# Two waits for GpSimd copies and thirteen matrix steps issued as 64-row pairs, in a sliding-window attention and gMLP kernel

## The chip, the cores and the metric

One core of one Trainium2 chip runs the whole program. The metric is device time in microseconds of an execution; a profiled execution gives a trace beside it. TensorE is called PE, VectorE DVE, ScalarE ACT, GpSimd POOL and SyncE SP, as in the profile.

## The reference

For each of 8 batch elements, q, k and v have 8 heads of 576 positions by 64. Attention is causal with a window of 64; its output, heads side by side, goes through a gMLP block with a spatial gate.

```python
scores = scale * np.matmul(q, k.transpose(0, 1, 3, 2))
mask = (rel >= 0) & (rel < window)                  # rel = query position - key position, window = 64
attn = softmax of the masked scores                 # along the keys
x = heads side by side of np.matmul(attn, v)        # (8, 576, 512)
h = np.maximum(x @ w_in, 0.0)                       # (8, 576, 1024)
u, v = h[..., :512], h[..., 512:]
v_n = (v - mu) / np.sqrt(var + 1e-06)               # layer norm of each row
v_s = np.einsum('ts,bsd->btd', w_spatial, v_n) + b_spatial[None, :, None]
return (u * v_s) @ w_out
```

## The kernel before

The kernel plans 1096 steps and issues them in the order of a list written out by hand, `ORDER` (L18 to L148). An entry such as `G1_3:PE:1` names a step, the engine that issues it and the buffers or PSUM banks that it takes. Steps of one engine run in the order of the list; semaphores from the tile framework order them across engines, by data and by the reuse of buffers and of the eight PSUM banks (128 rows by 512 float32 each).

For batch element b the steps are these, with g for the half of the heads and u for a pair of heads within it:

- `ldq`, `ldk`, `ldv` (DMA issues on SP) bring q, k and v; `cq`, `ck` (POOL, some on DVE or ACT) cast q and k to float16; `tq`, `tk` (DVE, L436) transpose them.
- `cv{b}_{lo}` casts two of the four 128-row chunks of v into the tile hv (L467). `sl` and `su` copy its lower and upper 64 rows into hs, v shifted by 64 rows (L474, L481). On POOL the helper `cp` (L298) issues one instruction of 512 elements a chunk (L308), so cv2_2 and su3_2 are two instructions each.
- `S` computes scores in products over 32 rows of the array (L512), `S{b}_r` those of the last 64 queries (L583); `E` exponentiates them on ACT (L521, L593), `M` masks them on DVE (L524, L597), `Z` sums them over the keys by products with a matrix of ones that write 64 output rows each (L537, L606), `N` and `n` form 1/sum on ACT as exp(-ln) (L563, L565), `P` multiplies with v in products of 64 output rows (L548, L619), and `X` multiplies by 1/sum on DVE (L556, L627) and writes x.
- `V` is x times the right half of w_in, `Vr` its ReLU on ACT (L677), `Vb` and `Va` its layer-norm statistics on DVE (L679, L681); `L1`, `L2` on ACT make 1/sqrt(var + eps), and five steps `A{b}_{j}` apply the layer norm on DVE (L736), in the order A1_4, A1_2, A1_3, A1_1, A1_0 and A2_1, A2_2, A2_0, A2_3, A2_4. `U` and `Ur` are the left half of w_in and its ReLU (ACT, L765), `G` the spatial product, `Ge` the gate on DVE (L796), `O` the product with w_out, `Oe` its eviction on ACT (L654), `st` the store.

V, U and O of an index below 4 are four products of 128 rows, 128 output rows and 512 columns, accumulated in one bank; G is five of them (the last has 65 rows: 64 of v and one for the bias). All of these go through one helper, `mm` (L312), and stand in the profile at L318. The remainder of 64 positions has steps of its own: `V{b}_4` (L710, L713) writes 64 output rows of V for one batch element and, in the other 64 rows of the same bank, the output product of the batch element before; `U{b}_4` is at L757 and `G{b}_4` at L788.

`mm` can issue a product in two ways; the list of before uses only the second:

```python
        if e == "PE2":
            for h in (0, 1):
                nc.tensor.matmul(o[64 * h:64 * h + 64, :], w[:, 64 * h:64 * h + 64], x, start=start, stop=stop)
        else:
            nc.tensor.matmul(o, w, x, start=start, stop=stop)
```

A second table, `HOLD` (L159), names steps whose first instruction waits, beside its own inputs, for the end of another step (L860). Before, it has one entry: sl6_0 on POOL waits for the mask M5_00 on DVE.

Of the kernel before, what the change touches and what calls it, by code (L numbers as in the profile page):

```python
# [55 lines left out]
A1_3:DVE:5 A1_1:DVE:6 A1_0:DVE:7 S2_1:PE:7:3:4:6 U1_2:PE:2 G1_2:PE:5 tk3_1:DVE:0 M2_01:DVE  # L56
M2_00:DVE E2_110:ACT:1 Oe0_3:ACT E2_100:ACT:3 E2_101:ACT E2_111:ACT M2_11:DVE st0_4:DQ ldq3_0:DQ:7
G1_1:PE:1 ldq3_1:DQ:1 S2_r:PE:4:0:7:3 Ur1_2:ACT:0 ldq4_0:DQ:2 ldk3_0:DQ:0 E2_r0:ACT:0 G1_4:PE:6
Z2_00:PE:2 E2_r1:ACT Z2_01:PE:4 E2_r2:ACT Ge1_1:DVE:5 M2_10:DVE G1_3:PE:1 G1_0:PE:0 Ge1_4:DVE:6
cv2_0:POOL:0 cv2_2:POOL sl2_0:POOL:0 su2_2:DVE sl2_2:DVE su2_0:POOL cq3_1:POOL:1 cq4_0:POOL:2  # L60
ck3_0:POOL:3 E2_r3:ACT N2_00:ACT:4 M2_r:DVE N2_01:ACT:2 n2_01:ACT s42:ACT n2_00:ACT Ge1_3:DVE:7
Ge1_0:DVE:8 cq3_0:POOL:0 st0_0:DQ Ge1_2:DVE:9 Z2_r:PE:7 Z2_10:PE:3 N2_r:ACT:5 n2_r:ACT P2_10:PE:6
P2_00:PE:2 P2_r:PE:4 P2_01:PE:1 X2_r:DVE:0 N2_10:ACT:0 n2_10:ACT Z2_11:PE:7 N2_11:ACT:3 P2_11:PE:0
n2_11:ACT O1_2:PE:5 V2_4:PE:3 Vr2_4:ACT:3 Oe1_4:ACT:0 X2_00:DVE:0 X2_01:DVE X2_10:DVE:1 X2_11:DVE
O1_3:PE:4 Oe1_2:ACT:0 Oe1_3:ACT tq3_1:DVE:1 tk3_0:DVE:2 V2_3:PE:2 V2_2:PE:7 Vr2_3:ACT:0
tq3_0:DVE:3 S3_1:PE:1:6:0:3 Vr2_2:ACT:2 E3_110:ACT:3 E3_111:ACT V2_0:PE:5 Vr2_0:ACT:6 V2_1:PE:4
E3_100:ACT:0 Vr2_1:ACT:4 S3_0:PE:2:7:0:3 Vb2_3:DVE:3 Va2_3:DVE Vb2_2:DVE:2 M3_11:DVE Vb2_0:DVE:1
# [5 lines left out]
Ur2_3:ACT:1 su3_0:POOL cv3_2:POOL su3_2:POOL E3_r0:ACT:1 E3_r1:ACT E3_r2:ACT Z3_10:PE:5 Z3_11:PE:6
Z3_00:PE:2 Oe1_1:ACT N3_10:ACT:1 ldv4_1:DQ sl3_2:POOL cq4_1:POOL:3 ldv4_4:DQ:1 ldk4_1:DQ:4
A2_3:DVE:3 A2_4:DVE ldv4_2:DQ:0 st1_0:DQ ldq5_0:DQ:6 U2_0:PE:0 Ur2_0:ACT:2 ldv4_3:DQ st1_4:DQ
ldk5_0:DQ:1 E3_r3:ACT N3_11:ACT:5 n3_11:ACT N3_00:ACT:4 cv4_0:ACT:0 G2_3:PE:4 G2_1:PE:3 n3_00:ACT
n3_10:ACT M3_01:DVE tq4_0:DVE:4 tk4_0:DVE:5 G2_2:PE:7 G2_0:PE:5 Ge2_3:DVE:0 M3_r:DVE Ge2_1:DVE:1
Z3_r:PE:0 P3_10:PE:1 Z3_01:PE:6 P3_00:PE:4 P3_11:PE:2 N3_r:ACT:2 Ge2_2:DVE:2 P3_01:PE:3 P3_r:PE:7
# [127 lines left out]
def kernel(  # L206
# [643 lines left out]
    for s, eng, banks in CHOOSE(plan):  # L850
# [42 lines left out]
```

## Time and profile before

| what | value |
|---|---|
| median of 3 runs | 197.49 us (197.48 to 197.74) |
| profiled execution, its own time | 196.44 us |
| span of its trace, first to last instruction | 194.7 us |
| granted TensorE clock, mean | 1.00 |
| instructions | 7039 |
| HBM read and written | 32.79 MB, 9.44 MB |

The profiled execution took 1.74 us more than its span. A row of a timeline has the start and the length in us, the engine, the line, what is written and read, the shapes, how many instructions were merged, and in brackets idle time before them with what ended it. A product's shape `128*64 128x512` has 128 rows of the array, 64 output rows and 512 columns; LDWEIGHTS (PEld) loads its weights. Matmul ends in the trace are modelled, so the prediction goes by their starts. A row of a chain has start, length, engine, tile and line.

### The profile page before, as it was taken

What the parts mean: (1) busy time and instruction counts of PE and PEld (TensorE: products, weight loads), DVE (VectorE), ACT (ScalarE), POOL (GpSimd) and SP (SyncE); (2) the same over time, 40 slices, a digit from 0 to 9 for tenths busy, and PEclk for the clock granted to TensorE, in tenths of its full rate; (3) what the DMA queues carried; (4) which work ended last, traced back from release to release, by engine and by line L of the source; (5) the groups of instructions that cost most, each with busy time, mean ns of one, the idle gap of its engine ahead of it and who ended that gap; (6) DMA issues with size and microseconds to landing.
All of it is one profiled execution on the core that took longest, in us unless ns stands there. A gap on an engine that the chain in (4) does not pass through costs nothing.

```text
span 194.7 us, 7039 instructions
## 1 busy us (share of the span) xinstructions
PE 184.9 (95%) x2955; PEld 99.2 (51%) x2955; DVE 167.1 (86%) x315; ACT 152.8 (78%) x326; POOL 94.0 (48%) x161
## 2 busy tenths in 40 slices
PE   7598999999999999999999999999999999999992
PEld 5475356464545454464446445654556454544450
DVE  5999899999999999999999989999986876448530
ACT  2079689898978899999999789987998977704642
POOL 4085856677669956549946890497400000000000
PEclk9999999999999999999999999999999999999999
DMA  6999999999999988999799958079205000007245
GB/s 202 362 202 374 392 395 210 310 411 261 202 347 305 297 253 221 363 357 353 167 251 303 284 167 251 20 174 288 82 26 198 3 0 3 2 0 238 112 175 205
DMA packets 49570, 42.68 MB, mean 219 GB/s; under 512 B 38593, under 2 KB 38849, under 8 KB 49538
## 3 DMA queue, kind: packets, MB, share of 16 engines
q1 hardware_dynamic: 49314, 41.90, 71.1%
q8 instruction: 23, 0.38, 0.9%
q10 hardware_dynamic: 224, 0.33, 0.5%
q14 instruction: 9, 0.07, 0.1%
HBM read 32.79 MB, written 9.44 MB: 217 GB/s over the span
## 4 chain that ended last, share of the span: by engine, by line
PE 57%; DVE 27%; SPq 7%; DMA 4%; issue 2%; POOL 1%; ACT 1%
PE bank L318 42%; DVE st L679 4%; DMA nq<-in_q_dram 4%; DVE vn L736 4%; DVE qT L436 4%; DVE kT L436 3%; SPq L452 3%; PE bank L512 3%; DVE e L524 3%; DVE x L556 3%; PE bank L548 2%; PE bank L710 2%; PE bank L537 2%; PE bank L788 2%; DVE g L796 2%
## 5 line engine op out<-in xcount | busy, mean ns | idle before, releaser
L521 ACT ACTIVATE e<-bank 128x512 f16<-128x512 f32 x64 | 34.7, 600 | 9.7 <-PE bank L512 8.8
L318 PE MATMUL bank<-wspT,vn 128*128 128x512 f16 (+1 forms) x160 | 38.6, 380 | 0.0
L796 DVE TENSOR_TENSOR g<-bank,ru 128x512 f16<-128x512 f32 (+1 forms) x40 | 24.4, 624 | 12.1 <-PE bank L318 8.8
L318 PE MATMUL bank<-x,win 128*128 128x512 f16 x128 | 31.5, 380 | 0.0
L318 PE MATMUL bank<-wout,g 128*128 128x512 f16 x128 | 31.3, 380 | 0.0
L318 PE MATMUL bank<-win,x 128*128 128x512 f16 x128 | 30.8, 379 | 0.0
L677 ACT ACTIVATE vs<-bank 128x512 f16<-128x512 f32 (+1 forms) x40 | 23.2, 604 | 9.0 <-PE bank L318 6.5
L308 POOL CAST hq<-nq 128x384 f16<-128x384 f32 x39 | 23.1, 630 | 13.6 <-DMA nq<-in_q_dram 11.3
L654 ACT COPY ob<-bank 128x512 f32<-128x512 f32 (+1 forms) x39 | 22.8, 596 | 8.1 <-PE bank L318 7.8
L679 DVE BATCH_NORM_STATS2 st<-vs 128x6 f32<-128x512 f16 (+1 forms) x40 | 25.7, 667 | 1.2 <-ACT vs L677 1.1
L308 POOL COPY hs<-hv 64x512 f16<-64x512 f16 x36 | 24.4, 702 | 4.3 <-ACT hv L300 2.1
L308 POOL CAST hv<-nv 128x512 f16<-128x512 f32 x26 | 17.3, 681 | 16.5 <-DMA nv<-in_v_dram 9.5
L765 ACT ACTIVATE ru<-bank 128x512 f32<-128x512 f32 (+1 forms) x40 | 21.4, 567 | 3.7 <-PE bank L757 2.0
L318 PEld LDWEIGHTS <-vn 128*128 128x128 f16 (+1 forms) x160 | 15.0, 97 | 18.2 <-DVE vn L736 0.5
L524 DVE TENSOR_TENSOR e<-e,mask 128x1024 f16<-128x1024 f16 x32 | 23.9, 763 | 0.3 <-ACT e L521 0.2
L556 DVE TENSOR_TENSOR x<-bank,lz 128x512 f16<-128x512 f32 x32 | 20.3, 676 | 2.6 <-ACT lz L565 2.0
L436 DVE STREAM_TRANSPOSE kT<-hk 128x576 f32<-128x576 f32 x16 | 19.8, 1239 | 0.4 <-POOL hk L308 0.4
L436 DVE STREAM_TRANSPOSE qT<-hq 128x576 f32<-128x576 f32 x16 | 19.8, 1239 | 0.4 <-POOL hq L308 0.2
L565 ACT ACTIVATE lz<-lz 128x512 f32<-128x512 f32 x32 | 19.9, 642 | 0.3
L308 POOL CAST hk<-nk 128x384 f16<-128x384 f32 x33 | 17.0, 551 | 4.7 <-DMA nk<-in_k_dram 4.4
L318 PEld LDWEIGHTS <-x 128*128 128x128 f16 x128 | 11.9, 98 | 14.3 <-DVE x L556 0.5
L563 ACT ACTIVATE lz<-bank 128x512 f32<-128x512 f32 x32 | 18.3, 607 | 0.7 <-PE bank L537 0.4
(87 smaller groups left out, 272.7 us busy)
## 6 DMA issues: line engine op xcount, KB each, us to landing
nq<-in_q_dram SPq DMA_DIRECT2D x16, 576.0 KB, 6.9
nk<-in_k_dram SPq DMA_DIRECT2D x16, 576.0 KB, 7.2
nv<-in_v_dram SPq DMA_DIRECT2D x32, 256.0 KB, 6.5
out_dram<-ob SPq DMA_DIRECT2D x14, 512.0 KB, 4.0
wi<-in_moe_w_in_dram SPq DMA_DIRECT2D x4, 512.0 KB, 7.6
ws<-in_moe_w_spatial_dram SPq DMA_DIRECT2D x2, 576.0 KB, 9.3
nv<-in_v_dram SPq DMA_DIRECT2D x8, 128.0 KB, 6.2
wo<-in_moe_w_out_dram SPq DMA_DIRECT2D x2, 512.0 KB, 6.6
```

The source lines that it names most:

```text
L308: nc.gpsimd.tensor_copy(o[:, lo:lo + step], i[:, lo:lo + step])
L318: nc.tensor.matmul(o, w, x, start=start, stop=stop)
L436: d = add(f"t{name}{b}_{g}", ("DVE", 1.09), key, lambda e: nc.vector.transpose(qt.t[:, :].rearrange("p (i j) -> p j i", j=18), h.t[:, :].b ...
L521: ex.append(add(f"E{b}_{g}{u}{w}", ("ACT", 0.475), key, lambda e, u=u, w=w: nc.scalar.activation(e2[u].t[:, w, :], sc[2 * u + w].t[:, :], ...
L524: mins.append(add(f"M{b}_{g}{u}", ("DVE", 0.602), key, lambda e, u=u: nc.vector.tensor_tensor(e2[u].t[:, :, :], e2[u].t[:, :, :], mask[:, ...
L556: lambda e, u=u, ob=ob, lz=lz: nc.vector.tensor_tensor(x.t[:, u, :], ob.t[:, :], lz.t[:, :], ALU.mult),
L565: c = add(f"n{tag}", ("ACT", 0.09 + 0.00083 * n), key, lambda e: nc.scalar.activation(lz.t[:, 0:n], lz.t[:, 0:n], AF.Exp, bias=0.0, scale= ...
L654: lambda e: (nc.vector.tensor_copy if last else nc.scalar.copy)(view(), m.t[rows, 0:n]),
L677: rl = add(f"Vr{b}_{j}", ("ACT", 0.476), key, lambda e: nc.scalar.activation(vs.t[0:jn, :], m.t[0:jn, :], AF.Relu), deps=[pv], acq=[vs], u ...
L679: s1 = add(f"Vb{b}_{j}", ("DVE", 0.595), key + 0.02, lambda e: nc.vector.bn_stats(st6.t[0:jn, 0:6], vs.t[0:jn, :]), deps=[rl], acq=[st6], ...
L765: lambda e, m=m, ru=ru, n=n: nc.scalar.activation(ru.t[:, 0:n], m.t[:, 0:n], AF.Relu), deps=[pu], acq=[ru], uses=[m])))
L796: lambda e, m=m, g=g, ru=ru, n=n: nc.vector.tensor_tensor(g.t[:, 0:n], m.t[:, 0:n], ru.t[:, 0:n], ALU.mult),
```

## The change

Two entries join `HOLD`: cv2_2, the cast of the second half of v of batch element 2, waits for A1_0, the last of the five layer-norm applications of batch element 1; and su3_2, the copy of the upper rows of that half for batch element 3, waits for A2_4, the last of batch element 2's. Both run on POOL and wait for DVE.

Thirteen steps change their engine word from PE to PE2, so that `mm` issues each product as two of 64 output rows, with 64 columns of the weights each and the same moving operand: four G steps (five pairs each) and nine V, U and O steps (four pairs each), 56 pairs for 56 products. TensorE issues 56 more products and 56 more weight loads. All thirteen stand next to steps Z, P or V{b}_4, which write 64 output rows, or next to others of the thirteen.

In the list the entries su3_2, sl3_2 and cq4_1 now stand behind A2_3 and A2_4, since the table needs the step that is waited for to be issued first. No engine's own order of steps differs. The cut diff, line breaks of the list left as they fall:

```diff
-Z2_00:PE:2 E2_r1:ACT Z2_01:PE:4 E2_r2:ACT Ge1_1:DVE:5 M2_10:DVE G1_3:PE:1 G1_0:PE:0 Ge1_4:DVE:6
+Z2_00:PE:2 E2_r1:ACT Z2_01:PE:4 E2_r2:ACT Ge1_1:DVE:5 M2_10:DVE G1_3:PE2:1 G1_0:PE2:0 Ge1_4:DVE:6
...
-n2_11:ACT O1_2:PE:5 V2_4:PE:3 Vr2_4:ACT:3 Oe1_4:ACT:0 X2_00:DVE:0 X2_01:DVE X2_10:DVE:1 X2_11:DVE
+n2_11:ACT O1_2:PE2:5 V2_4:PE:3 Vr2_4:ACT:3 Oe1_4:ACT:0 X2_00:DVE:0 X2_01:DVE X2_10:DVE:1 X2_11:DVE
...
-V3_3:PE:1 cv4_2:POOL ck5_0:POOL:2 tk5_0:DVE:2 Vb3_0:DVE:2 U3_2:PE:3 U3_1:PE:4 S4_r:PE:6:5:7:0
+V3_3:PE2:1 cv4_2:POOL ck5_0:POOL:2 tk5_0:DVE:2 Vb3_0:DVE:2 U3_2:PE2:3 U3_1:PE2:4 S4_r:PE:6:5:7:0
...
-cv6_0:POOL:0 sl5_0:POOL:1 U4_0:PE:4 V4_3:PE:7 Vr4_3:ACT:4 U4_1:PE:0 Vb4_3:DVE:2 U4_2:PE:2
-E5_r3:ACT M5_r:DVE G3_1:PE:6 Va4_3:DVE Ge3_1:DVE:9 Z5_10:PE:3 Z5_01:PE:5 Ur4_1:ACT:4 L14:ACT:0
+cv6_0:POOL:0 sl5_0:POOL:1 U4_0:PE2:4 V4_3:PE2:7 Vr4_3:ACT:4 U4_1:PE2:0 Vb4_3:DVE:2 U4_2:PE2:2
+E5_r3:ACT M5_r:DVE G3_1:PE2:6 Va4_3:DVE Ge3_1:DVE:9 Z5_10:PE:3 Z5_01:PE:5 Ur4_1:ACT:4 L14:ACT:0
...
-V6_3:PE:3 E7_111:ACT S7_r:PE:5:2:7:0 V6_1:PE:4 E7_r0:ACT:1 E7_r1:ACT Vr6_3:ACT:6 Vr6_2:ACT:0
-G5_0:PE:6 st4_0:DQ st4_1:DQ E7_r2:ACT Vr6_1:ACT:2 E7_r3:ACT sl7_2:DVE M7_11:DVE Z7_00:PE:5
+V6_3:PE:3 E7_111:ACT S7_r:PE:5:2:7:0 V6_1:PE2:4 E7_r0:ACT:1 E7_r1:ACT Vr6_3:ACT:6 Vr6_2:ACT:0
+G5_0:PE2:6 st4_0:DQ st4_1:DQ E7_r2:ACT Vr6_1:ACT:2 E7_r3:ACT sl7_2:DVE M7_11:DVE Z7_00:PE:5
...
-HOLD = {"sl6_0": "M5_00"}
+HOLD = {"sl6_0": "M5_00", "cv2_2": "A1_0", "su3_2": "A2_4"}
```

More of the change, by code (lines that the diff above doesn't have):

```diff
@@ L72 @@
 A2_0:DVE:2 Ur2_2:ACT:3 Ur2_1:ACT:5 U2_3:PE:2 O1_0:PE:6 O1_1:PE:7 S3_r:PE:0:4:3:1 Oe1_0:ACT:1
[L73 to L78, printed above, removed]
+Ur2_3:ACT:1 su3_0:POOL cv3_2:POOL E3_r0:ACT:1 E3_r1:ACT E3_r2:ACT Z3_10:PE:5 Z3_11:PE:6 Z3_00:PE:2
+Oe1_1:ACT N3_10:ACT:1 ldv4_1:DQ ldv4_4:DQ:1 ldk4_1:DQ:4 A2_3:DVE:3 A2_4:DVE su3_2:POOL sl3_2:POOL
+cq4_1:POOL:3 ldv4_2:DQ:0 st1_0:DQ ldq5_0:DQ:6 U2_0:PE:0 Ur2_0:ACT:2 ldv4_3:DQ st1_4:DQ ldk5_0:DQ:1
+E3_r3:ACT N3_11:ACT:5 n3_11:ACT N3_00:ACT:4 cv4_0:ACT:0 G2_3:PE:4 G2_1:PE:3 n3_00:ACT n3_10:ACT
+M3_01:DVE tq4_0:DVE:4 tk4_0:DVE:5 G2_2:PE:7 G2_0:PE:5 Ge2_3:DVE:0 M3_r:DVE Ge2_1:DVE:1 Z3_r:PE:0
+P3_10:PE:1 Z3_01:PE:6 P3_00:PE:4 P3_11:PE:2 N3_r:ACT:2 Ge2_2:DVE:2 P3_01:PE:3 P3_r:PE:7
 Ge2_0:DVE:3 N3_01:ACT:0 n3_01:ACT ck4_1:ACT:0 X3_10:DVE:2 X3_00:DVE:3 n3_r:ACT S4_0:PE:0:5:1:6
```

## The prediction

> **What bounds the kernel now.** I read the page first, then the chain that ended last, then what TensorE (PE) waits for, then single engines' timelines where PE waits.
>
> ```profile
> PE 184.9 (95%) x2955; PEld 99.2 (51%) x2955; DVE 167.1 (86%) x315; ACT 152.8 (78%) x326; POOL 94.0 (48%) x161
> PE   7598999999999999999999999999999999999992
> DVE  5999899999999999999999989999986876448530
> ```
>
> PE is busy in nearly every slice, VectorE (DVE) almost as much until three quarters of the span. The question is where one holds the other. The chain, thinned to the places that the change touches:
>
> ```profile
> 52.72 2.85 DVE vn L736 x5
> ...
> 56.73 1.71 DVE e L524 x3
> ...
> 61.38 0.65 DVE er L597
> ...
> 64.67 1.87 DVE x L556 x3
> ...
> 75.64 3.48 DVE vn L736 x5
> ...
> 84.60 0.61 DVE x L556
> ```
>
> Up to 85 us the chain runs through DVE, and both groups of five layer-norm applications (A1 and A2, L736) lie on it. From 85.25 us it runs on PE to the last evictions. Within the stretch of 48 to 85 us PE's timeline has two waits for DVE that a bracket names, this one at the softmax sums of batch element 2's remainder and one at S4_0 (85.25, below):
>
> ```profile
> 62.06 0.30 PE L606 MATMUL bank<-er,ones 128*64 128x128 f16 x4 [0.32 <-DVE er L597]
> ```
>
> So a microsecond taken from DVE before 85 us reaches the end if PE gets its inputs earlier. After 85 us only what shortens PE counts, as long as the other engines keep up.
>
> **The change part by part.**
>
> *Two holds.* What is an application worth beside GpSimd (POOL) and without it? Stretches of A1, A2 and A3 (columns: length, then PE, PEld, DVE, ACT and POOL busy):
>
> ```profile
> 52.50:55.56 3.06, 3.06 (x75) 1.45 (x73) 3.06 (x7) 2.47 (x6) 3.00 (x6) 1.00 1.02 301
> 75.50:79.12 3.62, 3.62 (x51) 1.62 (x50) 3.62 (x7) 3.62 (x10) 3.56 (x7) 1.00 0.80 226
> 98.05:99.76 1.71, 1.71 (x9) 0.78 (x8) 1.70 (x6) 1.71 (x5) 0.00 (x0) 1.00 1.31 244
> ```
>
> With POOL idle (A3) five take 1.7 us; with POOL busy throughout (A1, A2) they take about 3.0 and 3.55. The holds keep POOL out of four of A1's five (the cast before cv2_2 still meets the first) and all of A2: DVE saves about 3.06 - 1.70 - 0.1 = 1.25 us at A1 and 3.6 - 1.7 = 1.9 us at A2. POOL's order, and where the held copies go:
>
> ```profile
> 52.29 1.84 POOL L308 CAST hv<-nv 128x512 f16<-128x512 f32 x3 [0.71 <-DMA nv<-in_v_dram]
> 54.09 1.95 POOL L308 COPY hs<-hv 64x512 f16<-64x512 f16 x3
> 57.92 4.46 POOL L308 CAST hq<-nq 128x384 f16<-128x384 f32 x6 [1.88 <-DVE e L524]
> ...
> 75.16 2.85 POOL L308 COPY hs<-hv 64x512 f16<-64x512 f16 x4
> 77.97 2.12 POOL L308 CAST hq<-nq 128x384 f16<-128x384 f32 x3
> 82.19 1.09 POOL L308 COPY hs<-hv 64x512 f16<-64x512 f16 x1 [2.12 <-ACT hv L300]
> ```
>
> Behind cv2_2 on POOL stand sl2_0, su2_0 and the q cast of 57.92. From cv2_2's first cast (52.9) to 56.04 is 3.2 us; released at about 54.3 they end at about 57.5, inside the 1.88 us gap, so the q cast keeps its time. Behind su3_2 stand sl3_2 and one q cast, which end at 80.09; 1.8 us later they end near 81.9, still before the copy of 82.19, which waits for ScalarE (ACT). PE reads these v tiles only behind the sums that wait for M2_r (61.38 above) and, for su3_2, behind the G2 products (below, 83.1). The next load into the buffer that cv2_2 frees, ldv5_0, stands two batch elements later. The displaced copies are hidden on POOL.
>
> They are not hidden from DVE. In 54.3 to 57.5 DVE now runs a transpose, then the masks M2 (L524), which had POOL idle before:
>
> ```profile
> 56.58 1.86 DVE L524 TENSOR_TENSOR e<-e,mask 128x1024 f16<-128x1024 f16 x3
> ...
> 74.54 1.09 DVE L524 TENSOR_TENSOR e<-e,mask 128x1024 f16<-128x1024 f16 x1
> ```
>
> Alone a mask takes 0.6 us of DVE's time; M3_10 at 74.54, beside v casts and copies, takes 1.09 (1.02 to the next start). The masks would start at 55.35 instead of 56.58; two slowed by 0.4 eat 0.8 of the 1.25 us. The third also needs an exponential of ACT, which follows PE and does not move:
>
> ```profile
> 55.69 1.60 ACT L521 ACTIVATE e<-bank 128x512 f16<-128x512 f32 x3
> ```
>
> It ends at 57.29, so M2_11 starts at 57.35 at best, against 57.77: hold 1 gives at most 0.42 us, and if all three masks lose 0.45 it gives 1.25 - 1.35 = -0.1. I take 0.2 us. It passes through M2_r (61.38) to the sums on PE at 62.06, whose wait of 0.32 us is long enough, and on along DVE's chain.
>
> Hold 2 is worth what PE loses at the second wait:
>
> ```profile
> 78.60 4.50 PE L318 MATMUL bank<-wspT,vn 128*128 128x512 f16 x20
> ...
> 84.61 0.26 PE L512 MATMUL bank<-qT,kT 32*64 32x128 f16 x2
> 85.25 0.76 PE L512 MATMUL bank<-qT,kT 32*64 32x128 f16 x62 [0.39 <-DVE x L556]
> ```
>
> S4_0 starts two products at 84.61 and the rest at 85.25, because X3_10, which frees its second bank, ends at 85.21. DVE arrives 1.9 us earlier at what follows A2, less 0.4 if the displaced copies slow mask M3_01. The four G2 steps on PE (78.60) are late next: the last ends at 83.1, its gate takes 0.6, X3_10 0.7, done at 84.4, before 84.61. The whole 0.64 us goes; bounds 0.5 and 0.7.
>
> *Thirteen steps as two products of 64 output rows* (56 pairs for 56 full products). Where PE passes between full and 64-row products it pauses:
>
> ```profile
> 91.68 0.38 PE L710 MATMUL bank<-win,x 128*64 128x512 f16 x1
> 91.68 0.38 PE L713 MATMUL bank<-wout,g 128*64 128x512 f16 x1
> 91.89 0.38 PE L537 MATMUL bank<-e,ones 128*64 128x512 f16 x2
> 92.21 1.04 PE L318 MATMUL bank<-win,x 128*128 128x512 f16 x4
> 93.08 1.89 PE L318 MATMUL bank<-x,win 128*128 128x512 f16 x8
> ...
> 95.21 1.02 PE L318 MATMUL bank<-wout,g 128*128 128x512 f16 x4
> ```
>
> A pair (L710 with L713) starts together and the next 64-row pair (L537) follows after 0.21 us, as fast as one full product (four in 93.08 - 92.21 = 0.87). From L537 to the full product of 92.21 it is 0.32: a pause of 0.10 us. With V3_3, U3_2, U3_1 as pairs it falls away; the one into the scores S4_r that follow stays. Counted over the order, seven pauses go: two around G1_3 and G1_0, two around O1_2, one each at the groups V3_3.., U4_0..G3_1, and V6_1, G5_0: 0.7 us gross. What carries?
>
> Around G1 nothing: PE waits there for M2_r. O1_2: its 0.2 us ends at V2_3, the next row below, which starts 0.16 us after the last x of the chain's row of 64.67 (ends 66.54); 0.1 at most goes on, and I take 0. V3_3's group: the product after S4_r (95.21) waits for a bank that ACT frees:
>
> ```profile
> 66.70 1.89 PE L318 MATMUL bank<-win,x 128*128 128x512 f16 x8
> ...
> 94.57 1.07 ACT L677 ACTIVATE vs<-bank 64x512 f16<-64x512 f32 x2
> ...
> 123.46 0.41 DVE L627 TENSOR_TENSOR x<-bank,lz_r 128x256 f16<-128x256 f32 x1
> ...
> 154.56 0.84 PE L537 MATMUL bank<-e,ones 128*64 128x512 f16 x6
> ```
>
> The first of those two (half of 1.07, less their overlap) ends at about 95.16, 0.05 before PE starts, so that pause's 0.1 is taken back; 0. The U4 group's time runs into V5_4, which starts as the DVE product of 123.46 ends, behind a row of DVE work without gaps; 0, at most 0.1. Behind G5_0's pause (ahead of 154.56) no PE step waits as closely, so it counts: 0.11.
>
> Weight loads of 64 and of 128 columns (mean ns behind the bar):
>
> ```profile
> L710 PEld LDWEIGHTS <-x 128*64 128x64 f16 x32 | 3.0, 109 | 3.2 <-DVE x L627 0.5 <-issue 0.4 <-DVE x L556 0.4
> L318 PEld LDWEIGHTS <-x 128*128 128x128 f16 x128 | 11.9, 98 | 14.3 <-DVE x L556 0.5 <-issue 0.4
> ```
>
> [...]
>
> *Sum.* 0.2 + 0.64 + 0 + 0.11 = 0.95 us off. Against it: after 85 us DVE moves 0.85 us ahead of POOL, whose casts follow DMA landings, and may meet POOL anew; I take 0.05 off, bounds 0 and 0.6 (below). Net 0.9 us. The profiled execution took 196.44 us, 194.7 of span and 1.74 around it; it becomes 195.54. The median of the runs, 197.49, lies 1.05 above that execution; less 0.9 it is **196.6 us**.
>
> **The rivals.**
>
> 1. *The gains are given back.* Masks M2 lose 0.45 us each (hold 1: -0.1), and the later applications, now earlier, meet POOL. A3 is the place: POOL idles there now (0.00 above); its last work before that is a v cast:
>
> ```profile
> 96.86 0.60 POOL L308 CAST hv<-nv 128x512 f16<-128x512 f32 x1
> ...
> 99.99 1.25 PE L318 MATMUL bank<-wspT,vn 128*128 128x512 f16 x5
> ```
>
> Begun 0.85 us earlier than 98.05, A3's first application and the mask ahead of it meet this cast (up to 97.5); each can lose 0.3 to 0.4, and 0.2 us (99.76 to 99.99) is covered. That is 0.5 us lost, and a total of -0.1 + 0.64 + 0.11 - 0.5 = 0.15: 197.3 us. For it: every A beside POOL is slow. Against: the copies of that stretch were themselves slowed and may end earlier too. [...]
>
> 2. *The pauses stay.* If something other than the number of output rows makes PE pause, pairs change nothing: 0.2 + 0.64 - 0.05 = 0.8 off, 196.7 us. The unbroken step from L713 to L537 speaks against it.
>
> 3. *Slower: the two products of a pair do not run together.* Here both stream the same rows of the moving operand; in every pair of this trace they stream different ones. The place is PE after 85 us, where 42 pairs stand on the path. Fully one after the other costs 42 x 0.216 = 9.1 us, about 205.5 us net of the rest. It decides from about 1.2 / 42 = 0.03 us a pair, and passes the line of "slower" some 0.01 beyond. The near row, 0.21 for a pair, speaks against any of it.
>
> **How the numbers follow.** Forecast 0.66; rival 1 0.20; rival 2 0.07; rival 3 0.07. Forecast alone: gains of 0.42 + 0.7 + 0.11 + 0.2 = 1.4 give 196.1 us; -0.1 + 0.5 + 0.11 - 0.1 = 0.4 give 197.1. Rival 1 reaches 197.5, and a further gain from masks that are not slowed 195.9. Range 195.9 to 197.4; rival 3 and rival 1's end stay out. 0.2% (0.39 us) is about what a measurement of this kernel can tell from none. Faster by more: 0.95 of the forecast, 0.9 of rival 2, a quarter of rival 1: 0.74. Within: 0.15. Slower: rival 3 and the tail of rival 1: 0.11.
>
> **What the profile of the changed kernel would show.** A1's group near 1.8 us and A2's near 1.7 on DVE; POOL idle beside them and its q cast still near 57.9; masks of 56 us at 0.65 or 1.1 (hold 1's size); S4_0 unbroken, with no wait for x; pairs starting together every 0.216 us; no 0.10 pause at 92, 116 and 154 us, but new short PE waits at the products after S4_r and at V5_4. It would be wrong if S4_0 still waits, if a pair takes 0.24 us or more, or if A3 lasts well over 1.7 us.

## The result and the profile after

| kernel | median, us | runs | lowest to highest |
|---|---|---|---|
| before | 197.46 | 22 | 195.97 to 199.67 |
| changed | 196.57 | 22 | 195.06 to 198.04 |

The ratio of the changed kernel to the kernel before is 0.9953, with a 95% interval from 0.9931 to 0.9975: about 0.9 us less, as forecast (196.6). Here and below the ratio leaves out the slow runs, those more than 1.5% above the fastest of their kernel (for the changed kernel 198.04 and 198.00), while the median counts every run, so ratios and medians need not stand in the same order. Single runs of one kernel spread over 3 us, so a profile of one execution can lie anywhere in that spread: the first one of the changed kernel is of its longest run, 198.04 us (span 196.3), and was 0.82 us behind the profile before at 45 us already, ahead of the change's first step. This is why stages are compared below by their lengths, and why a second profile (e5_again, 196.31 us, span 194.6) stands beside it.

First the page and the chain of the changed kernel's first profile (start, length, engine, tile, line):

```profile
PE 185.9 (95%) x3011; PEld 101.7 (52%) x3011; DVE 166.5 (85%) x315; ACT 152.7 (78%) x326; POOL 93.8 (48%) x161
```

```profile
58.14 1.14 DVE e L524
...
59.88 0.97 DVE e L524
...
62.59 0.65 DVE er L597
...
99.18 2.21 DVE vn L736 x5
```

The groups A1 and A2 (L736) have left the chain of their stretch. In their place stand two masks of batch element 2 (L524), each over 1 us long, and at 99 us the group A3, which the chain before did not hold. The stretches of A1, A2 and A3 (length, then PE, PEld, DVE, ACT, POOL busy):

```profile
53.39:55.42 2.03, 2.03 (x71) 1.09 (x69) 2.03 (x7) 1.56 (x3) 0.59 (x1) 1.00 1.08 247
76.77:78.47 1.70, 1.70 (x41) 0.83 (x40) 1.70 (x7) 1.70 (x5) 0.00 (x0) 1.00 0.73 149
99.10:101.38 2.28, 2.17 (x11) 0.78 (x8) 2.28 (x7) 2.28 (x7) 1.17 (x2) 1.00 1.06 237
```

A1 takes 2.03 us instead of 3.06, and POOL is busy beside it only with the cast ahead of cv2_2. A2 takes 1.70 instead of 3.6, with POOL idle. A3 takes 2.28 instead of 1.71: POOL is now busy there for 1.17 us.

PE's timeline at the places that the prediction named (start, length, what is computed, number of products; in brackets the wait and what ended it):

```profile
63.28 0.30 PE L606 MATMUL bank<-er,ones 128*64 128x128 f16 x4 [0.97 <-DVE er L597]
...
85.81 0.77 PE L512 MATMUL bank<-qT,kT 32*64 32x128 f16 x64
...
92.62 0.38 PE L537 MATMUL bank<-e,ones 128*64 128x512 f16 x2
92.84 1.03 PE L316 MATMUL bank<-win,x 128*64 128x512 f16 x8
93.70 1.89 PE L316 MATMUL bank<-x,win 128*64 128x512 f16 x16
95.53 0.34 PE L583 MATMUL bank<-qT,kT 32*64 32x64 f16 x32
95.94 1.02 PE L318 MATMUL bank<-wout,g 128*128 128x512 f16 x4
...
101.43 1.04 PE L318 MATMUL bank<-wspT,vn 128*128 128x512 f16 x4 [0.16 <-DVE vn L736]
...
125.62 0.40 PE L710 MATMUL bank<-win,x 128*64 128x512 f16 x1 [0.31 <-DVE x L627]
...
155.09 1.25 PE L316 MATMUL bank<-wspT,vn 128*64 128x512 f16 x10
156.17 0.81 PE L537 MATMUL bank<-e,ones 128*64 128x512 f16 x6
```

Hold 2 did what was forecast: S4_0 (85.81) runs as one row of 64, where before it started two products and waited 0.64 us. The pairs too: eight 64-row products (92.84) take the 0.86 us of four full ones, and follow the sums at once, 0.22 after them. After S4_r the next product comes 0.41 us later instead of 0.30: that pause's gain is taken back there, as forecast. From G5_0 (155.09, ten products for five) to the sums (156.17) it is 1.08 us instead of 1.17.

Three rows went the other way in this profile: PE waits 0.97 us for M2_r ahead of the sums at 63.28, three times as long as before, at 101.43 it waits for A3, and at 125.62, ahead of V5_4, for X5_r. The second profile, at the same places:

```profile
61.86 0.30 PE L606 MATMUL bank<-er,ones 128*64 128x128 f16 x4 [0.18 <-DVE er L597]
...
84.73 0.77 PE L512 MATMUL bank<-qT,kT 32*64 32x128 f16 x64
...
99.48 1.25 PE L318 MATMUL bank<-wspT,vn 128*128 128x512 f16 x5
```

S4_0 is as short again. The wait for M2_r is 0.18 us, and A3 is waited for by nobody. What holds in every profile and what only in some is the question of the experiments.

### The profile page after: what moved, and what is told of

It reads as the page before. It is cut to its first block, busy times and chain, and to the rows that moved or that the text cites. A ratio compares the mean times of both kernels' runs of the same rounds, so it can differ in the third digit from the quotient of the medians.

```text
span 196.3 us, 7153 instructions
## 1 busy us (share of the span) xinstructions
PE 185.9 (95%) x3011; PEld 101.7 (52%) x3011; DVE 166.5 (85%) x315; ACT 152.7 (78%) x326; POOL 93.8 (48%) x161
## 4 chain that ended last, share of the span: by engine, by line
PE 66%; DVE 16%; SPq 7%; DMA 4%; ACT 2%; issue 2%; POOL 1%; DVEq 0%
PE bank L318 45%; DMA nq<-in_q_dram 4%; PE bank L512 4%; PE bank L316 4%; SPq L452 4%; DVE e L524 3%; DVE st L679 3%; PE bank L710 3%; PE bank L537 3%; PE bank L548 3%; DVE vn L736 2%; DVE qT L436 2%; PE bank L757 2%; PE bank L788 2%; SPq L342 1%
## 5 line engine op out<-in xcount | busy, mean ns | idle before, releaser
L318 PE MATMUL bank<-wspT,vn 128*128 128x512 f16 (+1 forms) x140 | 33.9, 380 | 0.2 <-DVE vn L736 0.2
L318 PE MATMUL bank<-wout,g 128*128 128x512 f16 x124 | 30.3, 380 | 0.1
L318 PE MATMUL bank<-win,x 128*128 128x512 f16 x116 | 27.7, 379 | 0.0
L308 POOL CAST hq<-nq 128x384 f16<-128x384 f32 x39 | 21.4, 585 | 12.7 <-DMA nq<-in_q_dram 12.1
L308 POOL CAST hv<-nv 128x512 f16<-128x512 f32 x26 | 17.9, 704 | 18.6 <-DMA nv<-in_v_dram 11.3
L318 PE MATMUL bank<-x,win 128*128 128x512 f16 x108 | 26.6, 380 | 0.0
L524 DVE TENSOR_TENSOR e<-e,mask 128x1024 f16<-128x1024 f16 x32 | 24.6, 782 | 1.0 <-ACT e L521 0.9
L318 PEld LDWEIGHTS <-vn 128*128 128x128 f16 (+1 forms) x140 | 13.1, 98 | 15.8 <-DVE vn L736 0.8
L308 POOL CAST hk<-nk 128x384 f16<-128x384 f32 x33 | 17.6, 570 | 4.2 <-DMA nk<-in_k_dram 3.9
L318 PEld LDWEIGHTS <-g 128*128 128x128 f16 x124 | 11.2, 98 | 13.1 <-DVE g L796 0.8
```

Source lines behind the costliest of these rows:

```text
L308: nc.gpsimd.tensor_copy(o[:, lo:lo + step], i[:, lo:lo + step])
L524: mins.append(add(f"M{b}_{g}{u}", ("DVE", 0.602), key, lambda e, u=u: nc.vector.tensor_tensor(e2[u].t[:, :, :], e2[u].t[:, :, :], mask[:, ...
```

## The experiments

The theory, as predicted: hold 2 takes away the wait at S4_0 (0.64 us), hold 1 gives 0.2 us, the pairs 0.11. The main rival, after the first profile: hold 1 loses, and the later applications meet POOL. All ratios below are to the kernel before, run on the same chip. Three chips were used (e1 to e4, e5 to e8, e9 to e12), so times of different groups are best compared by their distance from their own kernel before.

| kernel | hold 1 | hold 2 | pairs | median, us (runs) | before, us (runs) | ratio, 95% interval |
|---|---|---|---|---|---|---|
| e1_hold2_pairs | no | yes | 13 | 196.44 (12) | 197.33 (35) | 0.9981 [0.9946, 1.0015] |
| e2_hold1 | yes | no | 0 | 197.02 (12) | 197.33 (35) | 1.0010 [0.9975, 1.0045] |
| e3_hold2 | no | yes | 0 | 196.79 (12) | 197.33 (35) | 0.9997 [0.9961, 1.0034] |
| e4_pairs | no | no | 13 | 197.25 (12) | 197.33 (35) | 1.0028 [0.9993, 1.0063] |
| e5_again | yes | yes | 13 | 196.47 (12) | 197.00 (30) | 0.9960 [0.9934, 0.9985] |
| e6_apart | yes | yes | 13 + 9 | 199.03 (7) | 197.00 (30) | 1.0091 [1.0052, 1.0129] |
| e7_block | yes | yes | 13 + 9 | 196.82 (12) | 197.00 (30) | 1.0008 [0.9984, 1.0031] |
| e8_late_pairs | yes | yes | last 7 | 196.41 (12) | 197.00 (30) | 0.9981 [0.9954, 1.0009] |
| e9_hold2_late | no | yes | last 7 | 196.40 (12) | 197.31 (35) | 0.9965 [0.9933, 0.9996] |
| e10_no_v3 | no | yes | 10 | 196.61 (12) | 197.31 (35) | 0.9977 [0.9939, 1.0015] |
| e11_plus16 | no | yes | 13 + 4 early | 198.94 (12) | 197.31 (35) | 1.0094 [1.0061, 1.0128] |
| e12_minus12 | no | yes | 13 | 197.12 (12) | 197.31 (35) | 0.9991 [0.9959, 1.0024] |

The intervals are 0.2 to 0.4% wide to each side. They confirm the whole change twice (first result and e5_again) and hold apart what is worth 2 us; an edit of 0.2 us they cannot show. The times forecast for e2, e3 and e4 (0.2, 0.64 and 0.1 us off) are therefore neither confirmed nor refuted: their medians are 0.31, 0.54 and 0.08 us below the kernel before, and their intervals include 1. For those the lengths of stages have to do, from the first product of one step on PE to that of another, one profile of each kernel:

| profile | S2_r to Z2_r | Z2_r to Z3_00 | P3_r to V3_2 | V3_2 to U3_3 | U3_3 to Z4_10 | V4_4 to U4_0 | V6_1 to P7_01 | O0_2 to O7_4 |
|---|---|---|---|---|---|---|---|---|
| before | 4.17 | 15.32 | 3.04 | 11.71 | 2.03 | 1.97 | 2.72 | 146.00 |
| changed | 4.72 | 15.31 | 2.40 | 12.04 | 2.37 | 1.89 | 2.62 | 146.76 |
| e5_again | 3.93 | 15.65 | 2.40 | 11.71 | 2.03 | 2.18 | 2.61 | 145.64 |
| e1_hold2_pairs | 3.69 | 15.30 | 2.40 | 11.88 | 2.04 | 2.46 | 2.62 | 145.20 |
| e2_hold1 | 3.79 | 15.55 | 3.00 | 11.71 | 2.04 | 2.13 | 2.72 | 145.88 |
| e3_hold2 | 4.17 | 15.31 | 2.39 | 11.71 | 2.04 | 1.99 | 2.72 | 145.50 |
| e4_pairs | 3.66 | 15.32 | 3.03 | 11.71 | 2.04 | 2.97 | 2.62 | 146.43 |
| e6_apart | 4.67 | 15.32 | 2.39 | 11.76 | 2.04 | 2.16 | 2.62 | 148.04 |
| e7_block | 3.59 | 15.71 | 2.39 | 11.88 | 2.03 | 1.90 | 2.62 | 145.67 |
| e8_late_pairs | 4.10 | 15.32 | 2.40 | 11.74 | 2.57 | 1.90 | 2.62 | 146.80 |
| e9_hold2_late | 4.02 | 15.55 | 2.39 | 11.71 | 2.04 | 2.74 | 2.62 | 145.88 |
| e10_no_v3 | 3.87 | 15.74 | 2.40 | 11.71 | 2.03 | 1.89 | 2.62 | 145.48 |
| e11_plus16 | 3.97 | 15.53 | 2.40 | 13.47 | 2.04 | 1.89 | 2.62 | 149.16 |
| e12_minus12 | 3.66 | 15.93 | 2.40 | 12.18 | 2.03 | 1.91 | 2.62 | 146.26 |

Two columns are steady, and they are what the change surely brings: P3_r to V3_2, with S4_0's wait in it, is 2.39 to 2.40 us in all eleven profiles with hold 2 and 3.00 to 3.04 in the three without; V6_1 to P7_01 is 2.61 to 2.62 with the late pairs and 2.72 without. Together 0.74 us. The other columns vary from one execution to the next.

### The parts alone: e1 to e4

Each is the changed kernel with parts of the change taken back:

```diff
 e1_hold2_pairs
-HOLD = {"sl6_0": "M5_00", "cv2_2": "A1_0", "su3_2": "A2_4"}
+HOLD = {"sl6_0": "M5_00", "su3_2": "A2_4"}
 e2_hold1 (all PE2 back to PE)
+HOLD = {"sl6_0": "M5_00", "cv2_2": "A1_0"}
 e3_hold2 (all PE2 back to PE)
+HOLD = {"sl6_0": "M5_00", "su3_2": "A2_4"}
 e4_pairs (PE2 as in the changed kernel)
+HOLD = {"sl6_0": "M5_00"}
```

> The changed kernel without hold 1 (cv2_2 no longer waits for A1_0); hold 2 and the pairs stay. The prediction's step (hold 1 gains 0.2 us): the sums Z2_r start 0.2 us later than with hold 1, and the kernel takes 0.2 us more than the changed one, 0.7 us less than the kernel before (196.8 beside 197.46). The rival (hold 1 loses, because the displaced copies slow the masks, as the changed kernel's trace with Z2_r at 63.28 suggests): Z2_r about 0.4 us earlier against the steps ahead of it than with hold 1, and about 1.3 us less than the kernel before.

> The kernel before with hold 1 alone. The prediction's step: A1 in about 1.8 us on DVE, masks of 56 us at 0.6 to 1.0 us, Z2_r 0.2 us earlier than before, measured from the same point, 0.2 us off the time. The rival: A1 as short, but M2_00, M2_11 and what follows them slower, Z2_r 0.4 us later, and 0.4 us more than the kernel before.

> The kernel before with hold 2 alone. The prediction's step: A2 in 1.7 us, S4_0 without its wait for x, 0.64 us off the time (0.5 to 0.7). Rival 1 of the prediction: S4_0 without its wait, but A3's first applications meet the v cast on POOL, G3_2 on PE waits about 0.4 us for A3, and 0.2 us or less is left.

> The kernel before with the thirteen steps as pairs alone, no new hold. The prediction's step: pairs every 0.216 us, seven pauses of 0.10 us gone, of which 0.11 us reaches the end: 0.1 us off the time. The rivals: the pauses stay (0 off); the pauses all carry (0.7 off).

*e3, hold 2 alone.* PE and DVE at its place:

```profile
84.67 0.77 PE L512 MATMUL bank<-qT,kT 32*64 32x128 f16 x64
```

```profile
75.21 1.69 DVE L736 TENSOR_SCALAR vn<-vs,mv,ln 128x512 f16<-128x512 f16 x5
```

The group takes 1.69 us and S4_0 does not wait: 0.65 us off that stage, as predicted. Rival 1's loss at A3 is not in this profile (2.04 us from U3_3 to Z4_10, as before).

*e2, hold 1 alone.* DVE first, then POOL:

```profile
53.14 1.60 DVE L736 TENSOR_SCALAR vn<-vs,mv,ln 64x512 f16<-64x512 f16 x5
...
55.76 1.77 DVE L524 TENSOR_TENSOR e<-e,mask 128x1024 f16<-128x1024 f16 x2
57.90 0.69 DVE L524 TENSOR_TENSOR e<-e,mask 128x1024 f16<-128x1024 f16 x1 [0.36 <-ACT e L521]
```

```profile
54.80 1.17 POOL L308 CAST hv<-nv 128x512 f16<-128x512 f32 x2 [2.18 <-DVE vn L736]
55.92 3.14 POOL L308 COPY hs<-hv 64x512 f16<-64x512 f16 x3
59.13 2.12 POOL L308 CAST hq<-nq 128x384 f16<-128x384 f32 x3
```

The group is short, and then DVE stands idle for 0.36 us at M2_11, waiting for ACT's exponential: the bound that the prediction named (E2_111) is where most of A1's gain ends. What is left brings Z2_r 0.38 us earlier (3.79 against 4.17), of which 0.23 are given back before Z3_00. In the changed kernel's first profile the same hold went the other way. Its DVE and its POOL:

```profile
56.44 1.26 DVE L524 TENSOR_TENSOR e<-e,mask 128x1024 f16<-128x1024 f16 x2
58.14 1.14 DVE L524 TENSOR_TENSOR e<-e,mask 128x1024 f16<-128x1024 f16 x1 [0.44 <-ACT e L521]
...
59.80 1.05 DVE L524 TENSOR_TENSOR e<-e,mask 128x1024 f16<-128x1024 f16 x1
```

```profile
55.48 2.70 POOL L308 CAST hv<-nv 128x512 f16<-128x512 f32 x2 [1.49 <-DVE vn L736]
58.13 2.19 POOL L308 COPY hs<-hv 64x512 f16<-64x512 f16 x3
60.38 3.67 POOL L308 CAST hq<-nq 128x384 f16<-128x384 f32 x6
```

The starts agree to 0.01 us: cv2_2's first cast 0.14 us after the transpose ahead of the masks, the first mask 1.10 us after it. In e2 the casts win and take 1.17 us, and the two masks beside the copies 1.77. In the changed kernel the masks win: they take 1.26 us, and the casts 2.70 (the second alone 2.14). The copies then start 2.65 us after the first cast instead of 1.12 and lie on the third and the fourth mask (1.14 and 1.05 instead of 0.69), and the q cast starts at 60.38. The second cast takes 2.14 us in four of the six profiles with hold 1 (changed, e5, e6, e8), where S2_r to Z2_r takes 4.72, 3.93, 4.67 and 4.10 us, and 0.61 in the other two (e2, e7), where it takes 3.79 and 3.59. Whether hold 1 pays thus goes with which of the two engines is slowed there, and the starts do not tell which. With both sets in place (changed, e5, e6, e7) S2_r to Z2_r takes 4.72, 3.93, 4.67, 3.59; with the pairs and no hold 1 (e1, e4, e10, e11, e12) 3.69, 3.66, 3.87, 3.97, 3.66.

*e1* misses the rival's forecast: it is 0.89 us below its kernel before, as the changed kernel was in the first result, and not 1.3, although Z2_r comes earlier (3.69 us after S2_r, against 4.72 and 3.93 in the changed kernel's two profiles). Part of what it won there was lost at V4_4: 2.46 us to U4_0 instead of 1.9.

*e4, the pairs alone*, has the 0.1 us at V6_1 and Z2_r 0.5 us earlier, and loses 1 us at V4_4. Its timeline there:

```profile
109.97 0.38 PE L710 MATMUL bank<-win,x 128*64 128x512 f16 x1
111.02 0.40 PE L713 MATMUL bank<-wout,g 128*64 128x512 f16 x1 [0.67 <-issue]
```

The last two products of V4_4 are a pair that starts together in the profile before and in nine others (in e1, e5 and e6 they lie 0.54, 0.26 and 0.25 us apart). Here the second starts 1.05 us after the first, and the bracket names no engine: PE waited for nothing that the profile shows. This was no part of any theory, and the rest of the runs look at it too.

### A second profile, and the price of a pair: e5 to e8

```diff
 e5_again: the changed kernel
 e6_apart: the changed kernel and
-U6_0:PE:4 U6_2:PE:0 U6_3:PE:2 U6_4:PE:3 U6_1:PE:7
+U6_0:PE2:4 U6_2:PE:0 U6_3:PE2:2 U6_4:PE:3 U6_1:PE:7
...
 and V6_0 O5_1 O5_2 V7_2 G6_0 G6_2 G6_3 as PE2
 e7_block: the changed kernel and
 U6_1 V6_0 U7_2 O5_1 V7_1 O5_2 V7_3 V7_2 V7_0 as PE2
 e8_late_pairs: the changed kernel and
 G1_3 G1_0 O1_2 V3_3 U3_2 U3_1 as PE
```

> The changed kernel once more, for a second profile of it and more times. If the losses in its first profile (Z2_r 0.4 us late behind slowed masks, G3_2 0.34 us longer for want of A3) belong to the change, both come again. If they are the phase of one execution between GpSimd and VectorE, as the holds alone suggest (G1_0 to Z2_r 0.38 us shorter with hold 1 alone, A3 covered with hold 2 alone), at least one is gone: G1_0's step near 1.2 us instead of 2.2, G3_2's near 1.17 instead of 1.51. The time stays 0.9 us below the kernel before.

> The changed kernel, with nine more steps late in the list (U6_0, U6_3, V6_0, O5_1, O5_2, V7_2, G6_0, G6_2, G6_3) as pairs, each between two full steps: 39 more pairs and 18 more passages between full and 64-row products, where no other engine holds PE. The prediction's step (a passage costs 0.10 us, a pair as much as a full product): 1.8 us more than the changed kernel, 198.4 us. Its rival 2 (the pauses do not come from the number of output rows): no change, 196.6. Its rival 3 (the products of a pair run one after the other): 39 x 0.216 = 8.4 us more, 205. [...]

> The changed kernel, with nine adjacent steps of the same stretch (U6_1, V6_0, U7_2, O5_1, V7_1, O5_2, V7_3, V7_2, V7_0) as pairs: 36 more pairs, and only 2 more passages. The prediction's step: 0.2 us more than the changed kernel, 196.8. If it is the pairs and not the passages that cost in the run of nine steps apart, this kernel loses nearly as much as that one: 1.7 us. Rival 3: 7.8 us more.

> The changed kernel, with the first six of its thirteen pair steps (G1_3, G1_0, O1_2, V3_3, U3_2, U3_1) as full products again; both holds and the seven late pair steps stay. The prediction's step (those six bring nothing to the end): the time of the changed kernel, 196.6, within 0.1 us, and the sums' start after V3_3's group as late as with them. The rival (their pauses carry): 0.3 to 0.5 us more. A second question: in two of the three profiles with all thirteen PE stops for 0.54 to 1.05 us between two products of V4_4 with nothing that it waits for; if the count of PE instructions ahead of it sets that, V4_4's products run on here every 0.21 us, as in the kernels without pairs.

*e5* settles that the two losses of the first profile are not fixed parts of the change: G1_0's step is 1.43 us (2.21 there), G3_2's 1.17 (1.51). By the medians it is 0.53 us below its kernel before, not 0.9, by the ratio 0.8. A3's loss shows in two of eleven profiles with hold 2: the changed kernel's first (0.34 us, U3_3 to Z4_10) and e8 (0.54).

*e6 and e7* price the passages. Steps apart, then steps in a block:

```profile
161.88 1.03 PE L318 MATMUL bank<-x,win 128*128 128x512 f16 x4
162.84 1.05 PE L316 MATMUL bank<-win,x 128*64 128x512 f16 x8
163.82 1.04 PE L318 MATMUL bank<-x,win 128*128 128x512 f16 x4
```

```profile
162.62 1.03 PE L316 MATMUL bank<-x,win 128*64 128x512 f16 x8
163.48 1.03 PE L316 MATMUL bank<-wout,g 128*64 128x512 f16 x8
164.35 1.03 PE L316 MATMUL bank<-win,x 128*64 128x512 f16 x8
```

In the block a step of four pairs starts every 0.86 us, as four full products do; between full steps one takes 0.98, and the full step ahead of it 0.96. From P7_01 to O7_4, where every other profile but e7's has 35.14 or 35.15 us, e6 has 37.17 and e7 35.37: 2.03 / 18 = 0.113 and 0.23 / 2 = 0.115 us for each passage, nothing for the pairs. So the pauses come from the passages (rival 2 falls), the products of a pair with one moving operand run together (rival 3 falls), and the 0.10 of the prediction was 0.01 low. By its median e6 lost 2.6 us against e5 on the same chip, by its profile 2.0 in this stretch.

*e8*: the first six pair steps away, and the time stays (196.41 beside 196.47 for e5), as predicted. V4_4's products run on:

```profile
109.44 0.38 PE L710 MATMUL bank<-win,x 128*64 128x512 f16 x1
109.45 0.38 PE L713 MATMUL bank<-wout,g 128*64 128x512 f16 x1
109.66 0.38 PE L537 MATMUL bank<-e,ones 128*64 128x512 f16 x2
109.97 0.77 PE L512 MATMUL bank<-qT,kT 32*64 32x128 f16 x64
```

### Where PE stops: e9 to e12

Counting PE's products from the start, the stop of e1 and e4 stands ahead of the product of index 1887 in both (the count from 0), and the shorter ones of the first profile of the changed kernel (0.14 and 0.19 us, in S4_1 and U3_4) ahead of 1503 and 1631. These lie 128 and 256 apart. Each product comes with a weight load, 256 instructions for 128 products, and the page counts packets of instructions:

```profile
q8 instruction: 23, 0.38, 0.8%
```

That is 16.5 KB a packet, and 3011 products / 23 = 131. The theory: PE's code comes in blocks of 128 products, and it stops where the next block isn't there yet; the thirteen pairs put 26 products ahead of V4_4, and so moved a block's edge from S5_1 into V4_4. The rival: the stop belongs to V4_4.

```diff
 e9_hold2_late: e8_late_pairs without hold 1
 e10_no_v3: e1_hold2_pairs with V3_3 U3_2 U3_1 as PE
 e11_plus16: e1_hold2_pairs and
-V0_1:PE:1 ck1_0:POOL:0 V0_0:PE:3
+V0_1:PE2:1 ck1_0:POOL:0 V0_0:PE2:3
...
-V0_2:PE:0 Vr0_2:ACT:3 V0_3:PE:6
+V0_2:PE2:0 Vr0_2:ACT:3 V0_3:PE2:6
 e12_minus12: e1_hold2_pairs and
-NSPLIT = 18
+NSPLIT = 12
```

> The changed kernel without hold 1 and with the first six pair steps as full products again: hold 2 and the seven late pair steps. The prediction's step (hold 1 gains 0.2 us, the first six pairs nothing): 0.2 us more than the changed kernel, 196.7. The rival (hold 1 gains nothing, and what the first six pairs gain ahead of 85 us is lost at the stops of PE behind them): the time of the changed kernel, 196.5, with the sums Z2_r 2.65 us after G1_3's start as in the kernel before, and V4_4's products every 0.21 us.

> The changed kernel without hold 1 and with V3_3, U3_2, U3_1 as full products again: 12 products fewer ahead of V4_4 than in the kernel with hold 2 and all pairs. If PE's stops come every 128 products (there at products 1503, 1631 and 1887 of the kernels with all thirteen pairs), the one of V4_4 is gone (the 128th product then stands in S5_1), while G1_3 to V2_3 stay as short as with hold 2 and all pairs: 145.0 us from O0_2 to the last product O7_4's first, against 145.2 there, and 196.2 us. If V3_3's pauses carry, it is 0.2 us more instead.

> Hold 2 and all thirteen pairs, without hold 1, and with the four full V0 steps of the first batch element as pairs too: 16 products more at 23 us, no pause more. If the stops come every 128 products, none stands in V4_4 (product 1887 of the kernel) and the place of the stop moves 16 products ahead in the work: into S5_r. A stop, if there is one, is seen there, and at S4_r's end, not in V4_4 and U3_4. If the stops belong to V4_4 itself, it stops there again, by 0.3 to 1.05 us. The time is that of hold 2 with all pairs, 196.4, within 0.5.

> Hold 2 and all thirteen pairs, without hold 1, and with six of the warm-up steps at the start (D12 to D17) as two products of 512 columns instead of four of 256: as much work on PE, 12 products fewer. If the stops come every 128 products, V4_4 and U3_4 run on (0.887 and 0.466 us), the 128th product stands in S5_1, and the kernel takes 0.3 to 0.5 us less than with hold 2 and all pairs: 196.0 us, less than any kernel so far. If the stops belong to V4_4 itself: 196.4, with the stop there.

*e11* has the answer, and a price that neither theory gave. Its rows with a stop, but for one of 0.18 us in U2_4 at index 1247:

```profile
89.82 0.60 PE L318 MATMUL bank<-win,x 128*128 128x512 f16 x2 [0.59 <-issue]
...
96.29 0.23 PE L583 MATMUL bank<-qT,kT 32*64 32x64 f16 x6 [0.92 <-issue]
...
111.50 0.25 PE L583 MATMUL bank<-qT,kT 32*64 32x64 f16 x9 [0.73 <-issue]
...
153.06 0.59 PE L318 MATMUL bank<-win,x 128*128 128x512 f16 x2 [0.91 <-issue]
```

V4_4 runs on. The stops stand inside V3_0, S4_r, S5_r and V6_2, ahead of indices 1503, 1631, 1887 and 2654 (the edge would be 2655): 16 products earlier in the work than in the kernels with thirteen pairs, as the theory has it, but all four of about 1 us from start to start (0.97, 1.11, 0.92 and 1.29; Z6_01 to V6_1, with the last, takes 14.32 us beside 13.27 in e1). Sixteen products at 23 us that add no pause cost 2.5 us (198.94 beside 196.44 for e1). The expectation of "within 0.5" was wrong: I had moved the edges without asking what stands behind them. S steps issue 128 instructions in 0.7 us (64 products with their loads; S7_1 runs from 150.85 to 151.55 in e11), so a block that holds one of them lasts less time, and its successor may be late; this reading no run tests.

*e12* shifts the other way. U3_4 and V4_4 run on, as expected; the hoped-for 0.4 us do not come (197.12 us instead of 196.0): other edges now stop, at P2_00 and in S4_1 (indices 991 and 1503):

```profile
64.00 0.22 PE L548 MATMUL bank<-e,hs 128*64 128x64 f16 x2 [0.40 <-issue]
...
91.38 0.52 PE L512 MATMUL bank<-qT,kT 32*64 32x128 f16 x38 [0.28 <-issue]
```

*e9* has the edge where the kernel before has it, inside S5_1, and there it stops as well in this execution (1.54 us from S5_1 to U4_0, 0.77 before). Its time, 196.40, is nearer to its rival's 196.5 than to the 196.7 of the prediction's step, but 0.2 us is what these times cannot show, and Z2_r comes 2.50 us after G1_3, not 2.65:

```profile
111.46 0.55 PE L512 MATMUL bank<-qT,kT 32*64 32x128 f16 x41 [0.63 <-issue]
```

*e10* has no stop, its V4_4 to U4_0 is 1.89 us, and V3_2 to U3_3 stays at 11.71: V3_3's pauses carry nothing. It misses its other forecasts, 145.0 us from O0_2 to O7_4 by 0.5 and 196.2 us for the whole by 0.4 (196.61).

Over the fourteen profiles the timelines have ten rows from 46 us on that PE begins with a wait of "issue"; nine stand at an index of 95 + 128 n, and the tenth, e11's in V6_2, one product ahead of one. Ahead of 46 us there are four more, all at index 223 (Z0_11, in e2, e5, e8 and e10). So the place is settled. The trace's packet records add when: each of the ten ends 2.2 to 2.7 us after the start of a 16 KB instruction packet (the four 2.9 to 3.2), and no block in the fourteen profiles is entered sooner than 2.2 us after its packet's start. Why a packet starts late in one execution and not in another wasn't tried. In the two profiles of the changed kernel the stops took 0.3 us each time (S4_1 and U3_4; V4_4).

No kernel here beats the changed one by more than these measurements tell: e1, e5, e8 and e9 lie within 0.1 us of each other.

## Why the prediction was right, point by point

- *Hold 2, 0.64 us (0.5 to 0.7)*: right, in all eleven profiles: 0.60 to 0.65. The copies behind it on POOL were hidden, as argued.
- *V6_1 and G5_0, 0.11 us*: right, 0.10.
- *V3_3's group and the U4 group, 0 each*: right. After S4_r the next product comes 0.11 us later in the changed kernel's first profile (95.53 to 95.94), and e10 without V3_3's group as pairs has the same stage length as e4 with it. The U4 group's 0.1 went into the steps behind it, U4_0 to U4_4 being 5.31 us before and 5.24 to 5.59 in the profiles with these pairs.
- *O1_2, 0 (at most 0.1)*: right in the sum, not in the place. Of the two pauses counted there one goes (O1_2 to V2_4 0.86 us instead of 0.97); P2_11 to O1_2 stays at 0.37, since O1_2 starts 0.04 to 0.05 us after the end of a gate on DVE that it needs. The 0.11 us does not end at V2_3; it goes on to Z3_00, where PE then waits for ACT, 0.1 us longer in e1, e4 and the changed kernel.
- *A pair costs a full product, a passage 0.10 us*: right for the pair (e7), and 0.113 for the passage. The pairs' loads of 64 columns average 110 ns in the changed kernel's first profile against 98 for 128 columns, and e7's 36 extra pairs cost nothing: 0.23 us more from P7_01 to O7_4, which its two passages account for.
- *Hold 1, 0.2 us (-0.1 to 0.42)*: not borne out. The step that failed is "the displaced copies are hidden on POOL": they were given the 3.2 us that they take in the trace before, and take 4.3 to 5.7 in the six profiles with hold 1, since the masks slow POOL as POOL slows the masks: three copies beside masks take 3.14 us in e2 against 1.95 before, the second cast 2.14 in the changed kernel against 0.61 in e2, and the masks up to 1.14 against 0.67. The q cast is then late in its turn (60.38). The bound by ACT was right: M2_11 waits for E2_111 in all six (0.09 to 0.77 us). From S2_r to Z3_00 the kernels with both hold 1 and all pairs (changed, e5, e6, e7) take 20.03, 19.58, 19.99, 19.30 us, the five with the pairs and no hold 1 18.99, 18.98, 19.61, 19.50, 19.59, before 19.49. The 0.4 us between the two means is no proof of a loss: it rests on 20.03 and 19.99, the profiles of two of the longest executions (198.04 and 201.17 us), and the other two lie among the five. Without the early pairs the order is the other way, 19.34 and 19.41 with hold 1 (e2, e8) and 19.49, 19.48 and 19.57 without (before, e3, e9). The medians of e8 and e9, with and without it, are 196.41 and 196.40, but 0.59 and 0.91 us below the kernel before on their chips; the sign stays open.
- *Around G1_3 and G1_0, 0, because PE waits for M2_r*: not borne out either. With the pairs and no hold 1 the stage to Z2_r is 0.2 to 0.5 us shorter, and that is kept to Z3_00 in e1 and e4 but not in e10 to e12. Why it is shorter is not understood: M2_r takes 0.40 to 0.41 us in e2, e4, e8, e10 and e12 and 0.71 to 0.72 in the other nine, and one of two copies on DVE ahead of it 0.42 us in some profiles and 0.63 to 0.75 in others, both with the early pairs and without them; that the pairs cause it is not shown. Why it is not always kept the traces do show. In thirteen profiles Z3_00 starts 3.30 us after the start of batch element 2's step L1 on ACT (L724), which waits for DVE's last statistics, and between M2_r and these DVE has hardly a gap. From Z2_r to Z3_00 it is 15.31 or 15.32 us where the mask M3_11 takes 0.67 to 0.68, and 15.55 to 15.94 where it takes 0.90 to 1.10 beside copies and casts on POOL (e2, e5, e7, e9, e10, e12; in e12 with the stop at P2_00). In e11 (15.53) the stop in U2_4 lies there. The rows of e10, on DVE and on ACT:

```profile
70.83 1.10 DVE L524 TENSOR_TENSOR e<-e,mask 128x1024 f16<-128x1024 f16 x1
...
74.29 0.30 ACT L724 ACTIVATE ln<-mv,eps_t 128x5 f32<-128x5 f32 x1 [0.70 <-DVE mv L681]
```

So PE's own gains ahead of Z3_00 count only where DVE arrives earlier too.

- *Loss of phase after 85 us, 0.05 (0 to 0.6), and rival 1*: the mechanism is there as priced, 0.34 and 0.54 us at A3 against the 0.5 worked out, but in two of the eleven profiles with hold 2, so it is no fixed part of the change. A second place was not in the sum: P5_01 to V5_4 takes 0.73, 0.65 and 0.96 us in the changed kernel's first profile, e7 and e8, with PE waiting for X5_r on DVE, and 0.28 to 0.36 in the other eleven; the prediction expected only a short wait there.
- *Left out*: the 56 more products move the edges that come every 128 products, and PE stops at some of them, by 0.3 us in each profile of the changed kernel and up to 1.07 at V4_4 in e4.

So the sum came out right through its largest term; that it met the median to 0.03 us is luck, as far as these runs tell. Of the 0.89 us between the medians, 0.74 is steady and shown in every profile; hold 1 does not fill the rest as predicted, and what does is not settled, since the parts that vary between executions are as large as it is.

## What to carry to other kernels

Forecast first the wait that one step makes unbroken (here S4_0) and look for its stage length in several executions; here it was the only gain of half a microsecond that stood out of the scatter. When a copy is moved off one VectorE group, price it at its new place by what it meets there, not by its old length (hold 1's copies: 4.3 to 5.7 us here, 3.2 before). And when a change adds instructions to the engine that bounds the kernel, count where its code blocks may end afterwards: here, where PE stopped at edges 128 products apart, the same work cost 2.5 us more with sixteen harmless products ahead of it.

## What the runs showed of the hardware that was not expected

In some executions PE stopped for 0.2 to 1.1 us at an index of 95 + 128 n of its products, 2.2 to 3.2 us after the start of an instruction packet; the profile has 23 such packets of 16 KB (0.38 MB) for 3011 products, 131 products a packet. That PE's code arrives in blocks of 128 products with their loads, and that PE stops for a block that came late, is read from these numbers. The stops were short in the profiles of the changed kernel, 0.3 us each time, and about 1 us at four edges in e11.

Where masks on VectorE meet casts and copies on GpSimd, either can be the one that takes longer: of two executions with the same starts to 0.01 us, one had the second cast of cv2_2 at 0.61 us and two masks, the second beside a copy, at 1.77, the other the cast at 2.14 and the masks at 1.26. Masks of 0.67 us elsewhere take up to 1.14 there. The prediction had charged only VectorE for the meeting.
